# Moving one group's preparation earlier in a hand-ordered DeltaNet and maxout FFN kernel

## Chip, cores and metric

The kernel runs on one core of one Trainium2 chip. The metric is the time of one execution on the device, in microseconds (us). Three runs of the kernel before gave 530.14, 530.81 and 528.37 us; the median is 530.14.

## What is computed

The first part is a delta-rule attention: for each of 4 batches and 8 heads, a 48x48 state is read and updated over 768 time steps. Its output, reshaped to 3072 rows of 384, goes through a feed-forward block with three input matrices, the maximum of the three products, and an output matrix.

```
k_n = k / (norm(k) + 1e-06)
for t in range(S):
    y[:, :, t] = einsum('bhd,bhde->bhe', q[:, :, t], state)
    v_old = einsum('bhde,bhd->bhe', state, kt)
    state = state + bt * einsum('bhd,bhe->bhde', kt, vt - v_old)
x = y.transpose(0, 2, 1, 3).reshape(B * S, H * D)
h = maximum(maximum(x @ w1, x @ w2), x @ w3)
out = h @ w_out
```

The inputs q, k, v and beta are float32; the FFN weights arrive as 64-bit floats and are converted on the chip.

## The kernel before

**Tiling.** Time is cut into 12 chunks of 64 steps. Two chunks make a group (`m`, 0 to 5), and a group gives one FFN tile of 512 tokens. A chunk has two units (`n`, 0 to 23), one for each half of the batches. The diff works on group 2 (units 8 to 11, "the third group"), while group 1 (chunks 2 and 3, units 4 to 7) passes through its recurrence and the FFN runs on group 0.

**What a group needs.**

- `turn(n)` (L345): TensorE transposes k and q of a unit into PSUM (`p_t`), ScalarE copies them to a `kqt` tile (6 buffers). In the tables it is `t`; for a unit of group 1 the q half alone is `T`, and `queries` adds a `load_q(n + 3)` on SyncE (SP) behind it.
- `gram(n)` (L427): TensorE forms K K^T and K Q^T (`p_g`). VectorE masks the q part into `pt` (L422), then ScalarE copies the k part to `at` (L455), and `at` is written to DRAM as `at_d` by four DMAs (L468). For units 10 and 11 these are on POOL's queue, otherwise on SP's. It is `g` in the tables; the q part alone of units 4 to 7 is `P`. `pt`, `at` and the FFN's `h` tiles share 17 "square" buffers.
- `blocks(m)` (L510): one DMA on SP reads `at_d` back as `x_bl`, rearranged into 32x32 blocks, one for each partition.
- `solve(m)` (L521): a generator. Its first step takes the norms from the diagonal of `x_bl` (the root on ScalarE, L261; then VectorE, L262 to L266 and L281; L539 to L541), puts a scaled diagonal in place (POOL, L542) and scales `x_bl` (VectorE, L551). Then come 31 steps of forward substitution, each with one product (L565) and one difference (L569) on VectorE; then the result is written to DRAM as `y_d` (L591, SP) and read back as `ut` in two halves (L600). For group 1, `x_bl` and `y_bl` lie in the not yet used tile `wo_sb`, so the profile calls them that.
- The joins of a chunk: `turn_t1` (`d`, VectorE L632 and L634), `join_z` (`z`, TensorE p_z L709, ScalarE copies L712 and L714) and `join_u` (`j`, TensorE p_j L723, ScalarE L683).
- The recurrence: `old_k` (`k`), `old_q` (`q`), `new` (`u`, p_u L768), `step` (`s`), `to_y` (`y`), `to_x` (`x`).

**The FFN as clock.** `ffn(0)` is a generator of 31 pieces. Pieces 0 to 17 handle 256 tokens, pieces 18 to 26 handle 512: six matmuls each (p_h, L926), into one of two PSUM buffers, which are freed by a ScalarE copy (L934, every third piece) or a VectorE maximum (L940). Pieces 27 to 30 are the output products (p_o, L958). After each piece, the main loop (L1140 to L1178) issues what is listed for its number: weight fetches, `FIRST` (L1096), `EARLY_LINKS` (L1089), one weight conversion (`conv`: three ScalarE instructions L238 to L240, one on VectorE L250, one addition on POOL L254), some substitution steps, and loads. From group 1 on, other tables do the same.

**What sets the order.** The schedule is written by hand (`manual_schedule`, L96): each engine's instructions stand in its queue in the order of the program. Waits between engines are put in by the framework. So the place of a call in the loop fixes what it stands behind on each of the engines and DMA queues it uses. Within one piece the order is: fetches, the opening of `solve(2)`, `FIRST`, `EARLY_LINKS`, the conversion, further substitution steps, the loads, and `blocks(2)`.

Of the kernel before, what the change touches and what calls it, by code (L numbers as in the profile page):

```python
# [23 lines left out]
def kernel(  # L24
# [31 lines left out]
    nc = tc.nc  # L56
# [49 lines left out]
    both_queues = (nc.sync, nc.scalar)  # L106
    one_queue = (nc.sync, nc.sync)

    def rows(bb):
        return slice(C * bb, C * (bb + 1))  # L110
# [6 lines left out]
    def load(src, dst, n, queues):  # L117
        c, g = divmod(n, 2)
        for bb in range(2):
            queues[bb].dma_start(  # L120
                out=dst[rows(bb ^ g), :, 0:D],
                in_=src[2 * bb + g, :, c * C : (c + 1) * C, :].rearrange(
                    "h p d -> p h d"
                ),
            )
# [7 lines left out]
    def load_q(n, queues=one_queue):  # L133
        load(q, qpad[n % NQ], n, queues)

    def load_v(c, queue=nc.sync):
        vts[c] = work.tile([128, 2, H, D], FP32, name="v_t", bufs=3)
        for bb in range(2):
            queue.dma_start(  # L139
                out=vts[c][rows(bb)].rearrange("p g h d -> p (g h) d"),  # L140
                in_=v[2 * bb : 2 * bb + 2, :, c * C : (c + 1) * C, :].rearrange(
                    "b h p d -> p (b h) d"
                ),
            )
# [43 lines left out]
    t1 = [const.tile([128, 2, H, BL], FP32, name=f"t1{i}") for i in range(NU)]  # L188
# [286 lines left out]
    def in_rows(t):  # L475
        return t.rearrange("p s r -> p (s r)")[:, 0 : BL * BL].rearrange(
            "p (j i) -> p j i", i=BL
        )


    def in_wo(i):
        n = BL * BL + BL
        return wo_sb.rearrange("p t d -> p (t d)")[:, n * i : n * (i + 1)].rearrange(
            "p (s r) -> p s r", s=2
        )
# [35 lines left out]
    def solve(m):  # L521


        x = in_rows(xs[m])
        if m == 1:
            y_bl = in_wo(1)
        else:
            y_bl = work.tile([128, 2, HB * BL + HB], FP32, name="y_bl", bufs=1)
            if m > 2:
                zero = kpad[0][:, 0:1, D : D + 1]  # L530
                nc.scalar.copy(y_bl, zero.to_broadcast(y_bl.shape))
            else:
                nc.gpsimd.memset(y_bl, 0.0)
        y = in_rows(y_bl)
        bl = small("bl", BL)
        norm(bl, diagonal(x), small("root_bl", BL), small("nt_bl", BL))
        if m:
            norms_of(m, bl)
        nc.vector.reciprocal(bl, bl)  # L539
        nc.vector.tensor_tensor(out=bl, in0=bl, in1=bl, op=ALU.mult)  # L540
        nc.vector.tensor_tensor(out=bl, in0=bl, in1=beta_bl[:, m] if m else beta_0, op=ALU.mult)  # L541
        (nc.scalar.copy if m > 2 else nc.gpsimd.tensor_copy)(diagonal(y), bl)  # L542
        if m < FINE:
            size, xv, yv = HB, in_blocks(xs[m]), in_blocks(y_bl)
            xb = xv[:, :, :, 0:HB]
            by = bl.rearrange("p (s i) -> p s i", i=HB)[:, :, None, :]
            by = by.to_broadcast([128, 2, HB, HB])
        else:
            size, xv, yv = BL, x[:, None], y[:, None]
            xb, by = x, bl[:, None, :].to_broadcast([128, BL, BL])  # L550
        nc.vector.tensor_tensor(out=xb, in0=xb, in1=by, op=ALU.mult)  # L551
        yield
        for j in range(size - 1):
            a, b = j + 1, size - 1 - j
            n = BL // size
            tmp = work.tile([128, 256], FP32, name="tmp")
            t_v = tmp[:, 0 : n * a * b].rearrange("p (s c i) -> p s c i", s=n, i=b)
            row, column, rest = (
                xv[:, :, j, None, j + 1 : size],
                yv[:, :, 0:a, j, None],  # L560
                yv[:, :, 0:a, j + 1 : size],
            )
            if n == 1:
                row, column, rest, t_v = (t[:, 0] for t in (row, column, rest, t_v))
            nc.vector.tensor_tensor(  # L565
                out=t_v, in0=row.to_broadcast(t_v.shape),
                in1=column.to_broadcast(t_v.shape), op=ALU.mult,
            )
            nc.vector.tensor_tensor(out=rest, in0=rest, in1=t_v, op=ALU.subtract)  # L569
            yield  # L570
        if m == 0:
            back = in_rows(xs[0])
            nc.vector.transpose(out=back, in_=y.rearrange("p c i -> p i c"))
            yield
            for cc in range(2):
                for i in range(4):
                    bb, half = divmod(i, 2)
                    r = block(bb, half)
                    to = ut[cc][r, :, :, BL * half : BL * (half + 1)].rearrange(
                        "p g h i -> p (g h) i"  # L580
                    )
                    of = back[r, :, 16 * cc : 16 * (cc + 1)].rearrange("p i x -> p x i")
                    if half:
                        nc.scalar.copy(to, of)
                    else:
                        (nc.gpsimd if cc else nc.vector).tensor_copy(to, of)
                yield
            return
        y_d = dram.tile([2, 2, B, H, BL, BL], FP32, name="y_d")
        for cc in range(2):  # L590
            nc.sync.dma_start(  # L591
                out=y_d[cc].rearrange("f b h i j -> (f b h) i j"),
                in_=y[64 * cc : 64 * (cc + 1)],
            )
        yield
        for cc in range(2):
            for half in range(2):
                for bb in range(2):
                    r0 = C * bb + BL * half
                    (one_queue if m or cc else both_queues)[bb].dma_start(  # L600
                        out=ut[cc][
                            r0 : r0 + BL, :, :, BL * half : BL * (half + 1)
                        ].rearrange("p g h i -> p (g h) i"),
                        in_=y_d[cc, half, 2 * bb : 2 * bb + 2].rearrange(
                            "b h c i -> c (b h) i"
                        ),
                    )
            yield
# [363 lines left out]
    def some(gen, n):  # L972
        for _ in range(n):
            if next(gen, gen) is gen:
                break

    conv = weights()
    solving = solve(0)
# [96 lines left out]
    for n in (2, 3):  # L1075
        masked(pts[n], by_par(pts[n]))
    load_q(4)
    solving = solve(1)
# [8 lines left out]
        11: "u1 w0", 13: "y1 x1 s1", 14: "X0 w1", 16: "P0", 17: "X1 K0 K1 K2 K3",  # L1087
    }
    EARLY_LINKS = {  # L1089
        9: "k0 q0", 10: "t0", 11: "t1", 12: "g0", 13: "t2", 14: "g1", 15: "t3",  # L1090
        16: "g2", 17: "g3", 19: "d0 d1 z0 z1", 20: "j0", 21: "j1 u0", 22: "s0",
        24: "k1 y0 q1", 25: "u1 x0", 26: "s1", 27: "y1", 29: "x1",
    }


    FIRST = {  # L1096
        0: "f1 s0 S1 S1", 1: "z1 d1 S1 k1 S1 S1", 2: "j1 S1 S1 S1",
        3: "S1 q1 S1 S1", 4: "u1 T4", 5: "y1", 6: "s1 T5", 7: "x1 T6",
        8: "T7", 14: "P4", 15: "P5", 22: "P6", 23: "P7",
    }  # L1100


# [37 lines left out]
    for i, _ in enumerate(ffn(0)):  # L1140
        if 0 < i < 7:
            fetch(nc.sync)
        for _ in range(FETCHED.get(i, 0)):
            fetch(nc.gpsimd if i < 18 else nc.sync)
        if i == 25:
            some(conv, 1)
        if i == 20:
            solving = solve(2)
            some(solving, 1)
        if i == 21:  # L1150
            some(solving, 3)
        queries(FIRST.get(i, ""))
        links(1, EARLY_LINKS.get(i, ""))
        if i in CONVERTED:
            some(conv, 1)
        if 3 < i < 15:
            some(solving, (1, 1, 1, 1, 2, 3, 3, 3, 3, 3, 2)[i - 4])
        if i in (8, 12):
            prep_values(i // 4)
        if i in (1, 7):  # L1160
            for n in range(2):
                load_k(8 + 2 * (i > 1) + n, (nc.gpsimd, nc.gpsimd))
        if i in (1, 3):
            load_q(5 + i // 2)
        if i == 11:
            load_q(11, (nc.gpsimd, nc.gpsimd))
        if i in (3, 8, 10, 22):
            load_v((3, 8, 10, 22).index(i) + 2)
        if i == 18:
            blocks(2)  # L1170
        if i == 23:
            prep_values(4)
        if i > 21:
            some(solving, (3, 2, 3, 2, 2, 5, 5, 5, 4)[i - 22])
        if i in (27, 28, 29):
            load_blocks(i - 15, nc.sync)
        if i > 28:
            less_first(i - 29)  # L1178
# [5 lines left out]
    for m in range(1, GROUPS):  # L1184
        for i, _ in enumerate(ffn(m)):
# [8 lines left out]
            if m + 2 < GROUPS:  # L1194
                if i == 6:
                    blocks(m + 2)
                if i == 8:
                    solving = solve(m + 2)
# [32 lines left out]
```

## Time and profile before

| | |
|---|---|
| median of three runs | 530.14 us |
| the profiled execution | 529.45 us |
| its span in the profile | 527.7 us |
| mean granted TensorE clock | 0.966 |
| TensorE, VectorE, ScalarE, POOL busy | 94%, 59%, 31%, 35% of the span |
| pieces 0 to 17 of `ffn(0)` | 51.3 to 108.4 us |
| pieces 18 to 26 | 109.6 to 149.0 us |
| the output products of group 0 | 150.0 to 167.8 us |

The profile is one execution. Its times count from the span's start. A line of a timeline gives the start, the duration, the engine, the line of code, the instruction with its output and inputs, and how many were merged; what stands in brackets is the idle time of the engine before it and what is taken to have ended it. The chain of waits gives start, duration and instruction, followed back from the last. SPq is the queue of SyncE, which only issues DMAs here.

### The profile page before, as it was taken

How to read it: one execution, taken by the hardware profiler on the slowest of the kernel's cores; microseconds unless marked ns; L12 is line 12 of the kernel's file. 1: busy time of each engine (PE TensorE's matmuls, PEld its weight loads, DVE VectorE, ACT ScalarE, POOL GpSimd, SP SyncE). 2: the span in 40 equal slices, each digit the busy share in tenths (PEclk: the TensorE clock that was granted, in tenths of full speed). 3: DMA queues.
4: the chain of work that ended last, by engine and by line, in shares of the span. 5: the costliest groups of instructions: out<-in, count | busy, mean ns of one | idle time of the engine just before them, and what ended most of it. 6: DMA issues, size and time to landing. Idle time of an engine off the chain costs nothing.

```text
span 527.7 us, 18038 instructions
## 1 busy us (share of the span) xinstructions
PE 495.3 (94%) x7840; PEld 305.5 (58%) x7840; DVE 309.3 (59%) x695; ACT 164.5 (31%) x302; POOL 187.0 (35%) x308
## 2 busy tenths in 40 slices
PE   6666999798999999999999999999999999999996
PEld 6556678654565655556555665555565555654453
DVE  5877999946978664449662888654887231111100
ACT  5557576477311253110142201242201411011000
POOL 6515263653373668812195880501230000000000
PEclk9856899998999999999999999999999999999999
DMA  8974499466036865514594554833334202220011
GB/s 108 200 164 106 101 206 162 128 160 192 2 77 150 168 108 139 129 31 99 112 169 90 141 124 109 163 55 89 88 92 101 43 2 62 53 67 0 0 30 32
DMA packets 109055, 53.47 MB, mean 101 GB/s; under 512 B 91760, under 2 KB 102928, under 8 KB 108976
## 3 DMA queue, kind: packets, MB, share of 16 engines
q1 hardware_dynamic: 98704, 36.79, 33.6%
q0 software_dynamic: 8160, 15.13, 12.9%
q8 instruction: 62, 1.02, 0.8%
q10 hardware_dynamic: 2112, 0.39, 0.5%
q14 instruction: 17, 0.14, 0.1%
HBM read 39.17 MB, written 13.11 MB: 99 GB/s over the span
## 4 chain that ended last, share of the span: by engine, by line
PE 76%; DVE 13%; DMA 4%; ACT 3%; issue 2%; POOL 1%; SPq 0%; ACTq 0%; DVEq 0%
PE p_h L926 33%; PE p_o L958 25%; PE p_g L438 3%; DVE wo_sb L569 2%; PE p_u L768 2%; PE p_k L740 2%; DVE tmp L565 2%; PE p_q L740 2%; PE p_y L810 2%; PE p_s L791 1%; PE p_m L906 1%; DMA qall<-in_q_dram 1%; PE p_j L723 1%; DMA kpad<-in_k_dram 1%; PE p_z L709 1%
## 5 line engine op out<-in xcount | busy, mean ns | idle before, releaser
L926 PE MATMUL p_h<-xt,w_sb 128*128 128x512 f32 (+1 forms) x522 | 220.1, 566 | 9.0 <-DVE h L940 3.8
L926 PEld LDWEIGHTS p_h<-xt,w_sb 128*128 128x128 f32 x522 | 96.4, 194 | 95.7 <-issue 81.1
L958 PE MATMUL p_o<-wo_sb,h 128*128 128x384 f32 x288 | 97.7, 490 | 0.0
L940 DVE TENSOR_TENSOR h<-h,p_h 128x512 f32<-128x512 f32 (+1 forms) x48 | 29.7, 618 | 96.8 <-PE p_h L926 88.3
L958 PEld LDWEIGHTS p_o<-wo_sb,h 128*128 128x128 f32 x288 | 53.8, 190 | 36.0 <-issue 0.5
L964 ACT COPY o_sb<-p_o 128x384 f32<-128x384 f32 x24 | 11.5, 479 | 133.9 <-PE p_o L958 133.9
L565 DVE TENSOR_TENSOR tmp<-x_bl,y_bl 128x31 f32<-128x31 f32 (+20 forms) x139 | 50.3, 362 | 4.1
L569 DVE TENSOR_TENSOR y_bl<-y_bl,tmp 128x31 f32<-128x31 f32 (+20 forms) x139 | 49.2, 354 | 4.8
L936 ACT ACTIVATE h<-p_h 128x512 f32<-128x512 f32 x30 | 17.9, 597 | 91.3 <-PE p_h L926 83.9
L958 PE MATMUL p_o<-w_sb,xt 128*128 128x384 f32 x120 | 42.0, 486 | 0.0
L396 POOL DMA_DIRECT2D turned<-in_q_dram x72 | 39.1, 551 | 4.7 <-POOL turned L391 2.6
L438 PE MATMUL p_g<-kqt 48*64 48x64 f32 (+1 forms) x1216 | 27.3, 237 | 6.5 <-DVE nt_bl L263 3.8
L438 PEld LDWEIGHTS p_g<-kqt 48*64 48x64 f32 x1216 | 24.2, 137 | 13.9 <-ACT kqt L367 7.9
L958 PEld LDWEIGHTS p_o<-w_sb,xt 128*128 128x128 f32 x120 | 22.8, 190 | 15.9
L120 POOL DMA_DIRECT2D kpad<-in_k_dram x32 | 21.8, 689 | 24.9 <-PE p_s L791 23.9
L254 POOL TENSOR_TENSOR w_sb<-mant,up 128x384 int32<-128x384 int32 x18 | 18.2, 1009 | 30.2 <-DVE mant L250 17.1
L287 POOL TENSOR_TENSOR v_t<-v_t,nrm 128x768 f32<-128x768 f32 x12 | 17.9, 1495 | 25.8 <-DVE nrm L266 12.4
L798 DVE TENSOR_TENSOR st<-st,p_s 48x768 f32<-48x768 f32 (+1 forms) x18 | 17.1, 949 | 11.1 <-PE p_s L791 10.9
L812 DVE TENSOR_TENSOR y<-qs,p_y 128x768 f32<-128x768 f32 x11 | 10.5, 953 | 20.2 <-PE p_y L810 20.1
L391 POOL MEMSET turned<- 128x96 f32 x18 | 3.3, 191 | 47.2 <-DVE kqt L412 47.2
L139 POOL DMA_DIRECT2D v_t<-in_v_dram x12 | 9.9, 827 | 28.2 <-PE p_u L768 28.2
L752 DVE TENSOR_TENSOR v_t<-v_t,p_k 128x768 f32<-128x768 f32 x11 | 10.5, 951 | 15.9 <-PE p_k L740 15.9
(152 smaller groups left out, 624.3 us busy)
## 6 DMA issues: line engine op xcount, KB each, us to landing
w_bits<-in_moe_w_dram SPq DMA_DIRECT2D x14, 384.0 KB, 5.2
out_dram<-o_sb SPq DMA_DIRECT2D x48, 96.0 KB, 2.2
turned<-in_q_dram POOLq DMA_DIRECT2D x72, 48.0 KB, 2.8
kpad<-in_k_dram POOLq DMA_DIRECT2D x32, 96.0 KB, 5.3
y_x<-y SPq DMA_DIRECT2D x16, 192.0 KB
qall<-y_x SPq DMA_DIRECT2D x32, 96.0 KB, 2.7
ut<-y_d SPq DMA_DIRECT2D x40, 64.0 KB, 3.4
v_t<-in_v_dram SPq DMA_DIRECT2D x12, 192.0 KB, 6.1
```

The costliest lines, as they stand in the source:

```text
L120: queues[bb].dma_start(out=dst[rows(bb ^ g), :, 0:D], in_=src[2 * bb + g, :, c * C : (c + 1) * C, :].rearrange("h p d -> p h d"),)
L254: nc.gpsimd.tensor_tensor(out=dst.bitcast(I32), in0=mant_v.bitcast(I32), in1=up_v, op=ALU.add)
L287: nc.gpsimd.tensor_tensor(out=vts[c], in0=vts[c], in1=nrm[:, :, :, None].to_broadcast([128, 2, H, D]), op=ALU.mult,)
L396: (queue, nc.gpsimd)[i].dma_start(out=t[p0 : p0 + 32, bb, at : at + NP * 2 * D].rearrange("p (j x) -> p j x", j=NP), in_=(k, q)[i][2 * bb ...
L438: nc.tensor.matmul(p_g[rows(bb ^ (g * i)), par, c0 : c0 + C * (1 + whole)], kq[:, 0], kq if whole else kq[:, i],)
L565: nc.vector.tensor_tensor(out=t_v, in0=row.to_broadcast(t_v.shape), in1=column.to_broadcast(t_v.shape), op=ALU.mult,)
L569: nc.vector.tensor_tensor(out=rest, in0=rest, in1=t_v, op=ALU.subtract)
L740: nc.tensor.matmul(p_b[rows(bb), par, c0 : c0 + D], kqt[g][dims(par), j, bb ^ g, i], st[dims(par), bb ^ g, g, j],)
L926: nc.tensor.matmul(p_h, w_sb[i][:, t, f * 128 : (f + 1) * 128], xt[:, t, lo : lo + w], start=(t == 0), stop=(t == KT - 1),)
L936: nc.scalar.activation(out=h, in_=p_h, func=mybir.ActivationFunctionType.Relu)
L940: nc.vector.tensor_tensor(out=h, in0=h, in1=p_h, op=ALU.max)
L958: nc.tensor.matmul(p_o, stays, moves, start=(n == 0), stop=(n == len(terms) - 1))
```

## The change

Nothing is added to or taken from the computation: the same instructions are issued in another order, and one set of DMAs uses another queue.

- Group 1's `T` (transposes of q) and the loads of q move up: q5 and q6 to pieces 0 and 1, T4 to T7 from pieces 4, 6, 7, 8 to 2, 4, 5, 6, q11 from piece 11 to 8.
- Group 2's transposes move from pieces 10, 11, 13, 15 to 8, 10, 11, 13; its Gram products from 12, 14, 16, 17 to 10, 12, 14, 15; its block read from 18 to 16.
- Group 1's q products P4 to P7 move from pieces 14, 15, 22, 23 to 11, 19, 21, 22.
- `solve(2)` opens at piece 18 and not 20. Its steps: from three right after piece 21 and (3 2 3 2 2 5 5 5 4) from piece 22, to (2 2 2 2 3 3 3 3 5 5 4 1) from piece 19.
- The joins of group 1 and what follows them in the table move up by one piece, to 18 and on; `load_v(5)` from 22 to 21.
- Half of the reads of `ut` for group 1 go to POOL's queue; before, all eight are on SP's.

```diff
-                    (one_queue if m or cc else both_queues)[bb].dma_start(
+                    ((nc.sync, nc.gpsimd) if m == 1 else one_queue)[bb].dma_start(
...
     EARLY_LINKS = {
-        9: "k0 q0", 10: "t0", 11: "t1", 12: "g0", 13: "t2", 14: "g1", 15: "t3",
-        16: "g2", 17: "g3", 19: "d0 d1 z0 z1", 20: "j0", 21: "j1 u0", 22: "s0",
-        24: "k1 y0 q1", 25: "u1 x0", 26: "s1", 27: "y1", 29: "x1",
+        8: "t0", 9: "k0 q0", 10: "t1 g0", 11: "t2", 12: "g1", 13: "t3", 14: "g2",
+        15: "g3", 18: "d0 d1 z0 z1", 19: "j0", 20: "j1 u0", 21: "s0",
+        23: "k1 y0 q1", 24: "u1 x0", 25: "s1", 26: "y1", 28: "x1",
     }
...
     FIRST = {
-        0: "f1 s0 S1 S1", 1: "z1 d1 S1 k1 S1 S1", 2: "j1 S1 S1 S1",
-        3: "S1 q1 S1 S1", 4: "u1 T4", 5: "y1", 6: "s1 T5", 7: "x1 T6",
-        8: "T7", 14: "P4", 15: "P5", 22: "P6", 23: "P7",
+        0: "f1 s0 S1 S1", 1: "z1 d1 S1 k1 S1 S1", 2: "T4 j1 S1 S1 S1",
+        3: "S1 q1 S1 S1", 4: "T5 u1", 5: "T6 y1", 6: "s1 T7", 7: "x1",
+        11: "P4", 19: "P5", 21: "P6", 22: "P7",
     }
...
-        if i == 20:
+        if i == 18:
             solving = solve(2)
             some(solving, 1)
-        if i == 21:
-            some(solving, 3)
         queries(FIRST.get(i, ""))
         links(1, EARLY_LINKS.get(i, ""))
...
-        if i in (1, 3):
-            load_q(5 + i // 2)
-        if i == 11:
+        if i in (0, 1):
+            load_q(5 + i)
+        if i == 8:
             load_q(11, (nc.gpsimd, nc.gpsimd))
-        if i in (3, 8, 10, 22):
-            load_v((3, 8, 10, 22).index(i) + 2)
-        if i == 18:
+        if i in (3, 8, 10, 21):
+            load_v((3, 8, 10, 21).index(i) + 2)
+        if i == 16:
             blocks(2)
...
-        if i > 21:
-            some(solving, (3, 2, 3, 2, 2, 5, 5, 5, 4)[i - 22])
+        if i > 18:
+            some(solving, (2, 2, 2, 2, 3, 3, 3, 3, 5, 5, 4, 1)[i - 19])
```

## The prediction

> **What bounds the kernel now.** I read the page first, then TensorE's order of time with its idle spells, then VectorE, SyncE and the chain of waits around them. "Piece i" is the i-th step of the generator `ffn(0)`.
>
> ```profile
> PE 495.3 (94%) x7840; PEld 305.5 (58%) x7840; DVE 309.3 (59%) x695; ACT 164.5 (31%) x302; POOL 187.0 (35%) x308
> ```
>
> TensorE is busy 94% of 527.7 us. Of its idle time, only that between 58 and 127 us lies where the change works; from 131 us to the end it hardly stops (0.70, 0.34 and 0.37 us in all). So a delay of TensorE at 131 us is a delay of the end.
>
> ```profile
> 92.74 1.56 PE L926 MATMUL p_h<-xt,w_sb 128*128 128x256 f32 x6 [1.01 <-DVE h L940]
> ...
> 100.68 1.56 PE L926 MATMUL p_h<-xt,w_sb 128*128 128x256 f32 x6 [2.42 <-DVE h L940]
> ...
> 109.58 5.42 PE L926 MATMUL p_h<-xt,w_sb 128*128 128x512 f32 x12
> 114.93 1.37 PE L709 MATMUL p_z<-ut,at 32*32 32x32 f32 x128
> 116.44 2.81 PE L926 MATMUL p_h<-xt,w_sb 128*128 128x512 f32 x6
> 119.19 0.75 PE L723 MATMUL p_j<-z,t 32*32 32x32 f32 x64
> ...
> 126.81 3.35 PE L926 MATMUL p_h<-xt,w_sb 128*128 128x512 f32 x4 [2.29 <-DVE tmp L565]
> ```
>
> Counting the groups of six, 92.74 is piece 13, 100.68 piece 15, 109.58 pieces 18 and 19, 126.81 piece 22. Up to 103 us VectorE is behind: it shows no idle spell from 57 to 105 us, and the maxima that free PSUM stand in its queue behind the substitution of group 1. From 109.58 TensorE leads until the unexplained hole before piece 22.
>
> ```profile
> 107.01 4.88 SPq L600 DMA_DIRECT2D ut<-y_d  x8
> 111.94 0.96 SPq L215 DMA_DIRECT2D w_bits<-in_moe_w_out_dram  x2
> 117.96 0.33 SPq L515 DMA_DIRECT2D x_bl<-at_d  x1
> ```
> ```profile
> 112.97 1.65 POOL at_d L468 x3
> 114.63 3.27 DMA at_d<-at
> 117.90 0.02 SPq L515
> 117.96 3.84 DMA x_bl<-at_d
> 121.80 0.02 issue
> 121.83 0.27 ACT root_bl L261
> ```
>
> This is the chain that decides: the last Gram block of group 2 is copied by ScalarE at 110.56 (its row), written out by POOL, lands at 117.90, is read back, lands at 121.80; 11.2 us in all. Only then do `solve(2)`'s root and norms run.
>
> ```profile
> 116.33 0.69 DVE L940 TENSOR_TENSOR h<-h,p_h 128x512 f32<-128x512 f32 x1 [5.66 <-ACT h L934]
> 116.93 0.44 DVE L632 STREAM_TRANSPOSE t<-ut 128x256 f32<-128x256 f32 x1
> ...
> 122.12 0.18 DVE L262 TENSOR_SCALAR nt_bl<-root_bl 128x32 f32<-128x32 f32 x1 [1.42 <-ACT root_bl L261]
> ...
> 125.16 1.22 DVE L551 TENSOR_TENSOR x_bl<-x_bl,bl 128x1024 f32<-128x1024 f32 x1
> ```
>
> VectorE runs d0, d1 and the maxima of pieces 19 and 20 (to 120.7) before these norms. The wait for x_bl has little behind it.
>
> [...] TensorE reads `ut` at 114.93, so it had landed, yet its transpose on VectorE starts at 116.93, behind the maximum that waited 5.66 us. [...] after the 2.29 us hole the granted clock is 0.54 over 126 to 129 us; after the 2.42 us one at 100.68 it stayed 1.00. [...] Here 3.27 us for the last block's write, and SP stood until it landed. [...]
>
> **The change, part by part.**
>
> Front moves. T4 to T7, t0 and q5 to q11 go up one to three pieces. TensorE does the same work (0.44 us per 4 transposes). SP still interleaves these loads with weight fetches that wait for conversions; q4 and q5 were issued at 50.41 and 52.71, ten microseconds ahead of the new T4, so its data is there. POOL's q11 load (1.42 us) moves from 94.03 into POOL's idle 6.46 us before 89.35. I cost these at 0: VectorE's full queue to 103 us hides them. Without that cover the late q's would cost one load, 3 us.
>
> Gram work. Before, one masked pass (g0) stands in VectorE's queue ahead of the last step of `solve(1)`; after, three (g0, P4, g1). Two passes at 0.59 us from start to start: +1.18. The last step ends at 102.62 + 1.18 = 103.8, piece 15 starts near 101.8, y_d is issued 103.9. Behind it stand two passes instead of four: g2 at 104.0, g3 at 104.9. ScalarE copies g2's block near 104.7, then three conversions and h (1.9 us), then g3's near 107.1, against 108.67 and 110.56. P5 goes to piece 19; it was the one square buffer too many, so h of piece 18 no longer waits for the join (115.71). Pieces 16 to 18 (1.4, 1.4, 2.77 us, g3's 1.1 beside) end near 111.2 instead of 112.3: 1.1 us gained here.
>
> Queues. y_d lands 4.3 us after issue as before (102.68 to 107.01): 108.2. Half the `ut` reads now sit on POOL, between g2's and g3's writes. POOL: g2's four writes 105.2 to 107.7 (2.44), a conversion 1.0 to 108.7, four ut reads at about 0.6, no row for this pair, bounds 0.58 (L468) and 0.69 (q and k loads), I take 0.65: to 111.3; g3's writes 2.35 to 113.6. Landing: 2.0 to 2.7 us after the last issue's end (before 2.7, with two weight loads beside it): 116.1 taken at 2.5. x_bl: 3.0 to 3.84 us (4096-byte rows, alone then as now): near 119.6, bounds 118.5 to 122. So the read-back comes 2.2 us sooner, not two to four pieces. The ut reads land near 113 to 114, 1 us sooner than 114.9, but they are wanted at 111.2: p_z waits some 2 us, which lies inside the next wait and adds nothing.
>
> The added wait. `solve(2)` opens at piece 18, ahead of d0 d1 z0 z1 in the program. Its root therefore stands on ScalarE ahead of the z copies, its norms on VectorE ahead of d0 and d1, and ahead of the maxima of pieces 19 and 20. Behind the root: z copies (p_j waits for them), conversions, h of piece 21. Ahead of the root stand the conversions of pieces 16 and 17, which wait for POOL's add behind g3's writes (114.6), and h of piece 18: to about 118, hidden by x_bl. Behind the norms: d0 (p_j waits), d1, then the PSUM of piece 19. Root at 119.6, norms from root to the end of L551 126.38 - 121.83 = 4.5 us: 124.1; d0 (0.44 + 0.90) 1.4 us: p_j at 125.5. TensorE has only p_z, piece 19 and P5 for that time, done near 118: idle 7 us.
>
> Sum. I count to the end of piece 22's matmuls, before at 131.03. After: p_j 125.5, then j0 0.68, piece 20 2.77, j1 0.68, u0 1.08, pieces 21 and 22 5.54: 136.25. That is +5.2. The old 2.29 us hole and its half-clock piece (4.21 instead of 2.77) are in 131.03 and so given back already. [...] I take +1.7. P6, P7, s0, k1 and so on are the same work in another order: 0; VectorE has 12 steps instead of 9 in pieces 23 to 26 (0.85 us each), against a TensorE that is late, bound 0 to +2, taken 0. `load_v(5)`, one piece sooner on SP behind the fetches, 0 (needed a group later). At the end: the steps finish a piece sooner, so `less_first` runs in time for group 1's first matmul, which idled 0.70 at 168.44: -0.7. Total +6.2: 529.45 (the profiled execution, span 527.7) + 6.2 = 535.7. The median of the three runs is 530.14, 0.7 above that execution; I keep the smaller base.
>
> **Rivals.** (B) Milder: POOL keeps pace and loads land at their quickest, x_bl near 116.5. p_j at 122.4, +2.1, half clock +0.3 on average, -0.7: 531.2. For: ScalarE's copy is 3.5 us sooner. Against: POOL's ut reads stand in between. (C) Faster: x_bl is there by the end of piece 18, as the change means. Then the hole (2.29), its half clock (1.44) and the 0.70 go: 529.45 - 4.4 = 525.0. For: those waits exist. Against: the chain of 11.2 us would have to start near 100 us, and VectorE can't reach g3's mask before 104.9. (D) Worse than forecast: [...] x_bl at 122 (+2.4), VectorE's denser steps (+1): 541. C is the other side's: it decides from an x_bl landing before about 113 us; from 115 on the wait eats it.
>
> **Chances.** 0.5% of 530.14 is 2.65 us, about what a measurement of this kernel can tell from no change. Forecast 0.60 (533 to 539), B 0.15, C 0.10, D 0.15. Faster 0.10 (C), same 0.15 (B), slower 0.75. Leaving out C and the upper half of D, the range is 529.5 to 541.5.
>
> **What would show it.** Right: ScalarE's root waits for x_bl for some 2 us or more (from h of piece 18) with the z copies right behind it; VectorE idle until about 120, then norms, then L632; p_j about 125; TensorE idle 5 us or more after P5, then clock 0.5; POOL's four ut reads between the two groups of L468. Wrong: x_bl lands before 115; or p_z, p_j and piece 20 follow without a gap; or the time moves for something outside 85 to 175 us.

## The result

The kernel after takes 543.13 us (median of four runs, 541.52 to 543.98); the kernel before, with one more run beside it, 530.19 (528.37 to 530.81). The ratio is 1.0246, with a 95% interval of 1.0208 to 1.0284: the change makes the kernel 12.9 us slower. The prediction was 535.7 us with a range of 529.5 to 541.5, so the sign is right, but 543.13 lies outside the range, and less than half of the loss was foreseen.

The page of the kernel after, its first line of engines:

```profile
PE 502.4 (93%) x7840; PEld 309.9 (57%) x7840; DVE 309.5 (57%) x695; ACT 164.6 (30%) x302; POOL 189.9 (35%) x312
```

TensorE has the same 7840 matmuls and is busy 502.4 us instead of 495.3: so seven microseconds of the loss are the same work taking TensorE longer, at a mean granted clock of 0.952 instead of 0.966. Only POOL has more instructions, the four `ut` reads. The profiled execution took 543.98 us, its span is 542.3.

| in the profile, us | before | after | difference | predicted difference |
|---|---|---|---|---|
| first matmul of `ffn(0)` | 51.29 | 52.43 | +1.14 | 0 |
| VectorE's maximum of piece 10 | 88.58 | 89.74 | +1.16 | 0 |
| `y_d` issued | 102.68 | 108.05 | +5.37 | +1.2 |
| `x_bl` issued | 117.96 | 119.57 | +1.61 | -1.9 |
| `x_bl` landed (start + duration of the read) | 121.80 | 124.38 | +2.58 | -2.2 |
| first p_j of chunk 2 | 119.19 | 129.45 | +10.26 | +6.3 |
| end of piece 22 | 131.03 | 143.2 | +12.2 | +6.9 |
| group 1's first FFN matmul | 168.44 | 179.63 | +11.2 | +6.2 |
| group 2's first FFN matmul | 255.94 | 270.12 | +14.2 | +6.2 |
| profiled execution | 529.45 | 543.98 | +14.5 | +6.2 |

The end of piece 22 after is its end in the trace, 144.76, less 1.55 for P6 and s0, which now stand ahead of it. In the last prediction column 6.9 is 5.2 + 1.7, and 6.2 takes off the gap of 0.70. After group 2's first matmul nothing more is lost but 0.3 us.

The first row does not belong to the change. It stands ahead of every instruction that the change moves:

```profile
51.29 2.90 PE L926 MATMUL p_h<-xt,w_sb 128*128 128x256 f32 x6 [1.94 <-DVE xt L877]
```
```profile
52.43 1.53 PE L926 MATMUL p_h<-xt,w_sb 128*128 128x256 f32 x6 [1.26 <-DVE xt L877]
```

The upper line is before, the lower after. In the nine kernels below that keep the same start, this matmul stands between 51.04 and 52.84 us. So profiled executions differ by up to 1.8 us at this place already, and the 1.16 us of the second row are this same difference, carried along by VectorE's full queue.

TensorE of the kernel after in order of time, around the change (start, duration, instruction; idle time before it in brackets):

```profile
88.27 1.08 PE L438 MATMUL p_g<-kqt 48*64 48x128 f32 x27
92.59 0.44 PE L438 MATMUL p_g<-kqt 48*64 48x128 f32 x5 [3.23 <-issue]
...
118.77 1.06 PE L709 MATMUL p_z<-ut,at 32*32 32x32 f32 x60 [1.66 <-DMA ut<-y_d]
119.77 5.19 PE L926 MATMUL p_h<-xt,w_sb 128*128 128x512 f32 x6
...
129.45 1.90 PE L723 MATMUL p_j<-z,t 32*32 32x32 f32 x64 [3.87 <-DVE t L632]
131.27 4.56 PE L926 MATMUL p_h<-xt,w_sb 128*128 128x512 f32 x6
```

Three things are to be seen. In the middle of one Gram product, 27 matmuls done and 5 to go, TensorE stands 3.23 us, and the profile names no instruction that it waits for. Behind P5, ahead of the first p_j, it stands 3.87 us for VectorE's transposes. And pieces 19 and 20 take 5.19 and 4.56 us where a piece at full clock took 2.84 before. Piece 19 and P5 end near 125.6, though, and p_j has to wait for VectorE until 129.45 anyway, so the slow piece 19 only made that wait shorter and cost nothing by itself.

ScalarE, then VectorE of the kernel after, from the landing of `x_bl`:

```profile
124.40 0.26 ACT L261 ACTIVATE root_bl<-x_bl 128x32 f32<-128x32 f32 x1 [1.91 <-DMA x_bl<-at_d]
124.57 0.56 ACT L712 COPY z<-p_z 32x512 f32<-32x512 f32 x1
```
```profile
124.69 0.18 DVE L262 TENSOR_SCALAR nt_bl<-root_bl 128x32 f32<-128x32 f32 x1 [4.42 <-ACT root_bl L261]
...
128.86 0.44 DVE L632 STREAM_TRANSPOSE t<-ut 128x256 f32<-128x256 f32 x1
```

This is the predicted queue order, line for line: the root ahead of the z copies, the norms ahead of L632, and everything behind the landing of `x_bl`. Before, L632 stood at 116.93 and did not wait for it.

SyncE, then POOL of the kernel after:

```profile
108.05 1.15 SPq L591 DMA_DIRECT2D y_d<-wo_sb  x2
112.01 1.91 SPq L600 DMA_DIRECT2D ut<-y_d  x4
119.57 0.34 SPq L515 DMA_DIRECT2D x_bl<-at_d  x1
```
```profile
109.83 2.42 POOL L468 DMA_DIRECT2D at_d<-at  x4 [1.72 <-ACT at L455]
...
113.20 2.58 POOL L600 DMA_DIRECT2D ut<-y_d  x4
115.77 2.31 POOL L468 DMA_DIRECT2D at_d<-at  x4
```

POOL's order is also as forecast, with 0.645 us (2.58 by 4) for one `ut` read where 0.65 was taken; but its first line starts at 109.83 and not at 105.2. All these lines are of one execution: run 7 below has the same program up to its output pieces, and there the root starts at 123.12 and the first p_j at 128.17, 1.3 us sooner.

### The profile page after: what moved, and what is told of

It is laid out like the page before. It is cut to its first block, busy times and chain, and to the rows that moved or that the text cites. A ratio compares the mean times of both kernels' runs of the same rounds, so it can differ in the third digit from the quotient of the medians.

```text
span 542.3 us, 18031 instructions
## 1 busy us (share of the span) xinstructions
PE 502.4 (93%) x7840; PEld 309.9 (57%) x7840; DVE 309.5 (57%) x695; ACT 164.6 (30%) x302; POOL 189.9 (35%) x312
## 3 DMA queue, kind: packets, MB, share of 16 engines
q8 instruction: 62, 1.02, 0.8%
## 4 chain that ended last, share of the span: by engine, by line
PE 72%; DVE 10%; issue 5%; DMA 4%; ACT 4%; POOL 3%; SPq 2%; DVEq 0%; POOLq 0%; ACTq 0%
PE p_h L926 31%; PE p_o L958 22%; PE p_g L438 4%; PE p_u L768 3%; PE p_y L810 2%; PE p_s L791 2%; PE p_k L740 2%; PE p_m L906 1%; PE p_j L723 1%; PE p_q L740 1%; DVE wo_sb L569 1%; PE p_t L361 1%; DVE tmp L565 1%; DMA kpad<-in_k_dram 1%; DMA x_bl<-at_d 1%
## 5 line engine op out<-in xcount | busy, mean ns | idle before, releaser
L926 PE MATMUL p_h<-xt,w_sb 128*128 128x512 f32 (+1 forms) x522 | 222.7, 572 | 4.4 <-DVE h L940 1.5
L565 DVE TENSOR_TENSOR tmp<-x_bl,y_bl 128x31 f32<-128x31 f32 (+20 forms) x139 | 51.7, 372 | 4.1
L936 ACT ACTIVATE h<-p_h 128x512 f32<-128x512 f32 x30 | 17.9, 597 | 90.2 <-PE p_h L926 82.8
L438 PE MATMUL p_g<-kqt 48*64 48x64 f32 (+1 forms) x1216 | 29.8, 249 | 9.9 <-DVE nt_bl L263 3.8
L438 PEld LDWEIGHTS p_g<-kqt 48*64 48x64 f32 x1216 | 26.2, 148 | 18.9 <-issue 8.4
L422 DVE TENSOR_TENSOR pt<-p_g,mask 128x512 f32<-128x512 f32 x20 | 13.8, 688 | 12.1 <-PE p_g L438 12.1
## 6 DMA issues: line engine op xcount, KB each, us to landing
v_t<-in_v_dram SPq DMA_DIRECT2D x12, 192.0 KB, 12.6
```

The lines of the kernel that those rows point to most:

```text
L438: nc.tensor.matmul(p_g[rows(bb ^ (g * i)), par, c0 : c0 + C * (1 + whole)], kq[:, 0], kq if whole else kq[:, i],)
L565: nc.vector.tensor_tensor(out=t_v, in0=row.to_broadcast(t_v.shape), in1=column.to_broadcast(t_v.shape), op=ALU.mult,)
L926: nc.tensor.matmul(p_h, w_sb[i][:, t, f * 128 : (f + 1) * 128], xt[:, t, lo : lo + w], start=(t == 0), stop=(t == KT - 1),)
L936: nc.scalar.activation(out=h, in_=p_h, func=mybir.ActivationFunctionType.Relu)
```

## The experiments

**Theories.** Q: the loss is made by queue order; the norms of `solve(2)`, opened at piece 18, hold the joins until `x_bl` lands. F: it is made by the front; TensorE's spells marked "issue" and the later substitution delay `x_bl`. T: it is made behind 145 us, where the new list of steps puts DMAs of `solve(2)` on SyncE ahead of the next loads (the expectation of run 7 calls it the second part of Q). I, beside F: such a spell belongs to the place of an instruction in TensorE's stream, not to what it computes. Ratios are against the kernel before on the same chip; the runs were spread over several chips, so medians of different kernels are compared only roughly.

**1. The opening back at piece 20**, with before's list of steps.

```diff
-        if i == 18:
+        if i == 20:
...
+        if i == 21:
+            some(solving, 3)
...
-        if i > 18:
-            some(solving, (2, 2, 2, 2, 3, 3, 3, 3, 5, 5, 4, 1)[i - 19])
+        if i > 21:
+            some(solving, (3, 2, 3, 2, 2, 5, 5, 5, 4)[i - 22])
```

> The changed kernel, with only the opening of solve(2) and its steps put back to where they were before (opened at piece 20). Theory Q (the root and norms of solve(2) stand in ScalarE's and VectorE's queues ahead of the joins, so the joins wait for x_bl): p_j comes within 2 us of p_z and piece 19, near 124 instead of 129.45, no half-clock stretch after it, and y_d is again written behind the block loads; 533 to 535 us. Theory F (the loss comes from the front, where TensorE and VectorE are 5 us late by 108 us, and from the ut reads): 539 to 543 us.

Measured: 535.64 us, 1.0112 [1.0054, 1.0170], a little above what Q expected; 7.5 of the 12.9 us come back. The first p_j is at 124.15, group 1's FFN at 171.36. Of what remains, TensorE's waits for `ut` in p_z are a visible part (0.77 and 1.41 us before 117 us, and this one):

```profile
189.40 0.88 PE L709 MATMUL p_z<-ut,at 32*32 32x32 f32 x64 [1.81 <-DMA ut<-y_d]
```

**2. The opening at 18, but behind the joins of that piece.** The same instructions as after; the block that opens `solve(2)` stands two lines lower.

```diff
+        queries(FIRST.get(i, ""))
+        links(1, EARLY_LINKS.get(i, ""))
         if i == 18:
             solving = solve(2)
             some(solving, 1)
-        queries(FIRST.get(i, ""))
-        links(1, EARLY_LINKS.get(i, ""))
```

> The changed kernel, solve(2) still opened at piece 18, but behind d0 d1 z0 z1 of the same piece instead of ahead of them; its steps unchanged. Theory Q: z copies and d0 no longer wait for x_bl, p_j near 124; only the maximum of piece 19 still stands behind the norms (to 129), which costs about 1 us; the late end of group 1's loads stays: 535 to 538 us. Theory F: no change, 542 to 544 us.

Measured: 537.15 us, 1.0131 [1.0075, 1.0187], 6 us better than after. VectorE of this kernel:

```profile
120.61 0.43 DVE L632 STREAM_TRANSPOSE t<-ut 128x256 f32<-128x256 f32 x1
...
125.52 0.18 DVE L262 TENSOR_SCALAR nt_bl<-root_bl 128x32 f32<-128x32 f32 x1 [2.14 <-ACT root_bl L261]
```

Nothing but an order differs, L632 comes 8.2 us sooner (128.86 to 120.61), and group 1's FFN starts at 172.97 instead of 179.63. This is the cleanest proof of Q, and it also says that Q is not all: 4.5 us of delay are left at group 1's FFN (168.44 before), and some 3 us more are lost behind that point (below, 7).

**3. All `ut` reads on SyncE**, the rest as after.

```diff
-                    ((nc.sync, nc.gpsimd) if m == 1 else one_queue)[bb].dma_start(
+                    (one_queue if m or cc else both_queues)[bb].dma_start(
```

> The changed kernel with all eight reads of ut back on SP's queue. Theory Q with POOL's queue as its longest link: POOL writes the last Gram block some 2.5 us sooner, x_bl lands near 122 instead of 124.4, p_j near 127; ut lands 2 us later without cost: 540 to 541.5 us. If the reads on POOL don't matter: 543 us; if the later ut decides: 544 us or more.

Measured: 538.79 us, 1.0162 [1.0110, 1.0215], better than expected; the interval still touches that of the kernel after. POOL's second group of writes goes out at 112.88 instead of 115.77, `x_bl` is issued at 117.38 instead of 119.57, the root follows at 121.02 instead of 124.40, the first p_j at 126.50. So with the norms ahead of the joins, what delays `x_bl` delays the joins. Of the 3.4 us at the root, 2.2 come from the issue of the read; the other 1.2 come from a shorter read (3.64 us from issue to root, where after has 4.83), which this edit doesn't explain.

**4. The other way round: only the `ut` reads split, in the kernel before.** It is the diff of 3 reversed.

> The kernel before with only the ut reads split over SP and POOL. Theory Q: ut lands about 1.5 us sooner, where nobody waits for it, and POOL has its conversions and Gram writes 0 to 2 us later: 529.5 to 532 us, no difference that can be measured. If the split itself were a loss: 533 us or more.

Measured: 530.36 us, 1.0013 [0.9993, 1.0034]: no change. In its profile `x_bl` is issued at 120.44 instead of 117.96, and the time is the same: POOL's four reads cost nothing while nothing that waits for `x_bl` stands ahead of the joins.

**5 and 6. TensorE's stream shifted.** At the start, behind the warming matmuls, 32 small matmuls are added, whose product is used nowhere; once in the kernel before, once in after.

```diff
+    p_w = ps_ffn([128, TOK], "p_w")[0:32, 0:32]
+    for _ in range(32):
+        nc.tensor.matmul(p_w, ident[0:32, 0:32], ident[0:32, 0:32])
```

> The kernel before with 32 small extra matmuls into a scratch PSUM tile behind the warm-up matmuls, about 128 TensorE instructions, 0.5 to 1 us of work while TensorE waits for the first loads. It tests what ended TensorE's idle spell of 2.29 us ahead of piece 22. Theory I (TensorE ran out of instructions there, and the 16 KB fetches on the instruction queue fall at fixed places in its stream): the spell moves or shrinks with the places of the fetches, and the time changes by 1 to 4 us either way. Theory W (a wait on VectorE): the spell stays where it is, and the time is 530 to 531 us.

> The changed kernel with the same 32 small extra matmuls at the start. Theory I: the 3.23 us spell in the middle of unit 8's Gram products (27 of 32 matmuls done) goes from there, VectorE gets its mask at 89.7 instead of 93.1 and y_d is written about 3 us sooner; x_bl and p_j come up to 3 us sooner: 540 us, between 538 and 543 by where the next fetch falls. Theory W: the spell stays, 543 to 544 us.

Measured: 538.0 us (1.0124 [1.0082, 1.0166]) and 555.32 us (1.0458 [1.0424, 1.0492]). Both times missed what was expected. TensorE of the shifted kernel before:

```profile
42.72 1.49 PE L691 MATMUL p_f<-z,t 64*64 64x32 f32 x42 [3.70 <-issue]
```

The added matmuls alone took 3.62 us (at 4.86) where half a microsecond to one was expected, and the first matmul of `ffn(0)` stands at 58.05 instead of 51.29, or 56.91 instead of 52.43. In the kernel before this start is nearly all of the loss, so its time says nothing about the spells. The shifted kernel after lost 12 us by the medians (the profile is of the fastest execution, 549.88); beyond the 4.5 us at the start this stayed unexplained.

For theory I the places count. In before the large spells stood at 44.01 (0.97) and 58.95 (0.41); shifted, one of 3.70 us stands at 42.72. In after, shifted, the spell in unit 8's Gram product is gone; one of 1.15 us stands at 92.54 in p_q, and others of 0.83 and 1.59 us at 202 to 208 us. The count itself can be read from the traces. The spell of after comes behind 3,475 of TensorE's records (matmuls and weight loads), and so it does in all eight kernels here that have after's front, with 2.24 to 3.39 us. In both shifted kernels a spell (0.96 and 1.15 us) comes behind 3,477 records, though by the added matmuls other instructions stand there. So the place follows the count of TensorE's instructions, not the product that is computed. The size can't be told from this.

The hole of 2.29 us ahead of piece 22, which the first of these runs was to test, is not in the shifted kernel (0.91 and 0.29 us in its place). It is not in run 4 either, whose TensorE stream is that of before (0.32, 0.29 and 0.27 us), so it can't be laid to the shift; the forecast had counted this hole of one execution as given back.

**7. The last two numbers of the list of steps exchanged**, so that the write of `y_d` and the reads of `ut` come a piece later.

```diff
-            some(solving, (2, 2, 2, 2, 3, 3, 3, 3, 5, 5, 4, 1)[i - 19])
+            some(solving, (2, 2, 2, 2, 3, 3, 3, 3, 5, 5, 1, 4)[i - 19])
```

> The changed kernel with the last four yields of solve(2) (last step, y_d written, ut read in two halves) in piece 30 instead of 29, so behind the loads of unit 14's blocks on SP's queue, as before. Theory Q's second part (those loads now stand behind the y_d write and the ut reads on SP; VectorE waits 3.1 us for them in group 1's FFN and its join transposes come late): the idle spells of 1.04 us at 199.8 and the half-clock stretch behind them go: 540 to 541 us. If that order doesn't matter: 543 us.

Measured: 541.82 us, 1.0210 [1.0184, 1.0236], 1.3 us better than after by the medians, but the two intervals overlap. SyncE of the kernel before, then SyncE of the kernel after and what follows on its VectorE and on its TensorE:

```profile
166.38 3.86 SPq L396 DMA_DIRECT2D kmore<-in_k_dram  x8
...
171.54 2.42 SPq L591 DMA_DIRECT2D y_d<-y_bl  x2
175.33 4.88 SPq L600 DMA_DIRECT2D ut<-y_d  x8
```

```profile
182.95 6.64 SPq L600 DMA_DIRECT2D ut<-y_d  x8
189.69 3.77 SPq L396 DMA_DIRECT2D kmore<-in_k_dram  x8
```
```profile
194.92 0.45 DVE L412 STREAM_TRANSPOSE kqt<-kmore 128x256 f32<-128x256 f32 x1 [1.77 <-DMA kmore<-in_k_dram]
```
```profile
199.77 0.21 PE L723 MATMUL p_j<-z,t 32*32 32x32 f32 x2 [0.54 <-DVE t L632]
...
202.65 4.54 PE L926 MATMUL p_h<-xt,w_sb 128*128 128x512 f32 x6
```

The reads of k, 23 us later than before where group 1's FFN is 11 us later, hold VectorE 1.77 us here and 1.30 us at 196.67; behind them stand the join transposes; TensorE idles 1.04 us in three bits (0.54, 0.25, 0.25), and the piece behind these runs at a mean granted clock of 0.61 (4.54 us instead of 2.84). With the two numbers exchanged, `kmore` is issued at 178.57 and these lines are gone, but `ut` is read later and p_z waits 1.57 us for it at 196.34. From group 1's first FFN matmul to group 2's it takes 87.50 us before, 90.49 after, 88.69 here: 1.8 of T's 3.0 us. The same stretch is 90.2 to 90.5 us in kernels 2, 3 and 8, which keep after's list of steps, and 87.2 in 9 and 10, which keep before's list and before's joins.

The list of steps alone does not make the tail, though. Kernels 1 and 11 have before's list, but the joins a piece sooner, and take 88.8 and 91.4 us; there p_z waits for `ut` as in this run. In these three kernels `y_d` is issued 5.8 us behind group 1's first FFN matmul, in before, 9 and 10 only 3.1 us. So the moved joins have a part in the tail, and no run has them without the rest.

**8. Unit 8's Gram product ahead of unit 9's transposes.**

```diff
-        8: "t0", 9: "k0 q0", 10: "t1 g0", 11: "t2", 12: "g1", 13: "t3", 14: "g2",
+        8: "t0", 9: "k0 q0", 10: "g0 t1", 11: "t2", 12: "g1", 13: "t3", 14: "g2",
```

> The changed kernel with the two calls of piece 10 swapped (unit 8's Gram products ahead of unit 9's transposes; no instruction more or less). If TensorE's 3.23 us spell is a missing block of instructions at a fixed place of its stream, it now falls 70 instructions behind piece 10 as before, which is inside the transposes, and VectorE has its mask before it: y_d near 105 instead of 108, x_bl near 121.5, p_j near 126.5: 539.5 to 541.5 us. If the spell comes from the Gram products themselves: 543 us.

Measured: 541.79 us, 1.0209 [1.0176, 1.0242]. The spell did not go with g0; it now stands in the transposes:

```profile
92.12 0.37 PE L361 MATMUL p_t<-ident,kpad 128*128 128x128 f32 x1 [2.36 <-issue]
```

`y_d` is issued at 107.10 instead of 108.05; 105 was expected. A second finding for I: other instructions in the same place of the stream (behind the same 3,475 records), a spell again.

**9. The front of the change alone.** Kernel after with the parts of 1 and 3 undone, the joins, P6, P7 and `load_v(5)` at before's pieces, and P5 at 20.

```diff
-        15: "g3", 18: "d0 d1 z0 z1", 19: "j0", 20: "j1 u0", 21: "s0",
-        23: "k1 y0 q1", 24: "u1 x0", 25: "s1", 26: "y1", 28: "x1",
+        15: "g3", 19: "d0 d1 z0 z1", 20: "j0", 21: "j1 u0", 22: "s0",
+        24: "k1 y0 q1", 25: "u1 x0", 26: "s1", 27: "y1", 29: "x1",
...
-        11: "P4", 19: "P5", 21: "P6", 22: "P7",
+        11: "P4", 20: "P5", 22: "P6", 23: "P7",
```

> The changed kernel's early part alone (T4 to T7, q loads, group 2's transposes, Gram products and block read, P4 and P5), with joins, solve(2), its steps, P6, P7, load_v(5) and the ut reads at the places of before (P5 in piece 20). Theory Q: no root and no norm stands ahead of a join, so what remains is VectorE's late y_d (5 us): p_z waits 2 to 3 us for ut: 531 to 533.5 us. Theory F (the early part is where the loss comes from): 538 us or more.

Measured: 532.08 us, 1.0044 [1.0019, 1.0069]: slower by 2.2 us. TensorE of this kernel:

```profile
91.67 0.44 PE L438 MATMUL p_g<-kqt 48*64 48x128 f32 x5 [2.79 <-issue]
...
105.15 2.93 PE L926 MATMUL p_h<-xt,w_sb 128*128 128x256 f32 x6 [2.75 <-DVE h L940]
...
124.74 0.75 PE L723 MATMUL p_j<-z,t 32*32 32x32 f32 x64
```

The spell is there, and a wait of 2.75 us for VectorE's late maximum follows, behind which the piece takes 2.93 us where 1.56 was taken at 97.63, and the 64 Gram matmuls behind it 2.05 us (1.22 at 96.48). The wait of p_z for `ut` that was expected did not come. The first p_j does not wait for the norms (no bracket).

**10. The opening alone.** Kernel before with only `solve(2)`'s first step at piece 18 and `blocks(2)` at 17.

```diff
-        if i == 20:
+        if i == 18:
             solving = solve(2)
...
-        if i == 18:
+        if i == 17:
             blocks(2)
```

> The kernel before with only the opening of solve(2), its first step, moved from piece 20 to piece 18, and the block read from piece 18 to 17 so that it is issued ahead of it; steps from piece 21 on as before, joins at piece 19 as before. Theory Q: the joins' copies and transposes stand behind root and norms, p_j near 127.5 instead of 119.2, TensorE idle 7 us before it and at half clock after: 534 to 537 us. Theory F: 530 us.

Measured: 538.98 us, 1.0146 [1.0110, 1.0183], 9.1 us above before by the medians and 2 us more than Q expected. ScalarE, VectorE, TensorE of this kernel:

```profile
122.52 0.26 ACT L261 ACTIVATE root_bl<-x_bl 128x32 f32<-128x32 f32 x1 [4.63 <-DMA x_bl<-at_d]
```
```profile
122.81 0.18 DVE L262 TENSOR_SCALAR nt_bl<-root_bl 128x32 f32<-128x32 f32 x1 [10.55 <-ACT root_bl L261]
...
127.58 0.44 DVE L632 STREAM_TRANSPOSE t<-ut 128x256 f32<-128x256 f32 x1
```
```profile
128.17 0.28 PE L723 MATMUL p_j<-z,t 32*32 32x32 f32 x2 [7.32 <-DVE t L632]
```

The whole chain of the prediction in its pure form: ScalarE waits for the DMA, VectorE for ScalarE, TensorE for VectorE, 7.32 us in one hole, and then a granted clock of 0.50 (125 to 135 us).

**11. Three parts undone together** (1, 3 and 8), the joins still one piece sooner than before.

> The changed kernel with three things at once: solve(2) and its steps at the places of before, all ut reads on SP, and Gram products ahead of the transposes in piece 10; joins one piece sooner as in the change. Theory Q: what is left is the wait of p_z for ut (y_d 2 to 3 us late, the join a piece early), some 3 us: 531 to 534 us. If the three parts don't add up: 535 us or more.

Measured: 536.73 us, 1.0119 [1.0070, 1.0168], no better than 1 alone, and not the 531 to 534 that Q expected. Its TensorE waits 2.41 us for `ut` at 189.93, and the piece behind that wait takes 4.35 us instead of 2.84 (at 191.13); its spell in p_t is 3.24 us. So the parts don't add up, and why was not settled.

## Why the prediction was wrong in size

The forecast for the profiled execution was +6.2 us, and +14.5 came. Of the missing 8.3 us, 4.0 are there at the first p_j of chunk 2 (129.45 instead of 125.5), 1.3 more at the end of piece 22, and 3.0 come between the first FFN matmuls of groups 1 and 2. The mechanism that the forecast put first, the joins behind the norms, was right; the steps below had the wrong size or were not counted.

The parts were also measured by themselves: +9.1 for the opening (run 10), +2.2 for the front (run 9), and 1.3 that run 7 gave back. Their sum, 12.6, is near the 12.9 of the medians, but that doesn't prove that the parts add. Run 1 undoes the opening and the list of steps and should then stand 2.2 us above before; it stands 6.2 above (535.64 to 529.45), and run 11 is no better. What both keep and run 9 does not are the joins, P5 to P7 and `load_v(5)` one piece sooner; what these cost was not measured by itself.

**What held.** That the place of the opening is the largest part, and how: root ahead of the z copies, norms ahead of d0, d1 (runs 2 and 10). The two masks at +1.18. POOL's order, and 0.65 us for a `ut` read. p_z's wait for `ut`: some 2 us were forecast, 0.73 + 1.66 came. That the wait of p_z lies inside the next one and adds nothing: piece 19 and P5, behind it, end near 125.6, and p_j stands until 129.45. Rival C, the faster one, was tied to `x_bl` landing before about 113 us; it landed at 124.4.

**Right by luck, or not at all.** The gap of 0.70 us at group 1's first matmul went, but not for the reason given (that the steps finish sooner). In before that matmul waits for ScalarE's copy of an output:

```profile
168.44 2.81 PE L926 MATMUL p_h<-xt,w_sb 128*128 128x512 f32 x6 [0.70 <-ACT o_sb L964]
```

The gap is gone in runs 1 and 11 too, whose steps are those of before, and stays 0.70 in runs 9 and 10, whose joins are those of before. So, as far as these runs show, it goes with the moved joins. And `h` of piece 18, which was to come by 118, comes at 121.92, behind conversions that wait for POOL (before, 115.71); the landing of `x_bl` hides it, as the forecast said.

**First failed step: "near 119.6, bounds 118.5 to 122" for the landing of x_bl.** It is 124.4, beyond the upper bound. 3.5 us of the 4.8 are there when the read is issued (119.57, where the forecast's 2.5 us of landing gave 116.1), and they begin with the last substitution step: `y_d` is issued at 108.05, not at 103.9. Of these 4.15 us, 1.16 are the later start of this execution, which the change didn't make. Some 3 are the spell in unit 8's Gram product, which VectorE's mask has to wait for:

```profile
93.08 0.69 DVE L422 TENSOR_TENSOR pt<-p_g,mask 128x512 f32<-128x512 f32 x1 [2.92 <-PE p_g L438]
```

The forecast said of the front moves "I cost these at 0: VectorE's full queue to 103 us hides them", and counted the two masks at +1.18 with no wait. The cover was real for all that TensorE does late, except for g0: VectorE's queue has the mask of g0 right behind the maximum of piece 10, and so VectorE itself waits for TensorE. The rest, 1.3 us, is the read: 4.81 us where some 3.5 was taken. "Alone then as now" was wrong for both kernels; SyncE issues weight fetches right behind it, four before (3.84 us) and five after while the read is under way. Their number doesn't decide: in runs 3 and 7, with five as well, it is 3.6 and 3.7 us from issue to root. So this 1.3 us is spread of one execution as far as the runs show; without it, as in run 7, the landing of about 123.1 is still beyond the bound by 1.1 us, 0.9 of which are the later start of that execution.

**Second: half clock, counted at +1.7.** The 1.7 was the author's estimate. Stretches of the kernel after (us from : to, length, busy of TensorE, its loads, VectorE, ScalarE, POOL, granted clock, DMA share, GB/s), and the same of before:

```profile
118.00:124.80 6.80, 6.03 (x66) 2.78 (x66) 0.67 (x2) 3.77 (x9) 3.95 (x5) 0.52 0.65 214
128.00:135.00 7.00, 5.31 (x69) 2.98 (x70) 6.46 (x14) 2.73 (x5) 2.09 (x2) 0.52 0.06 21
202.70:207.10 4.40, 4.40 (x9) 1.81 (x8) 0.72 (x3) 1.18 (x2) 0.61 (x2) 0.61 0.48 84
```
```profile
126.50:130.00 3.50, 3.19 (x4) 1.44 (x5) 2.37 (x8) 2.43 (x5) 1.84 (x2) 0.55 0.60 107
```

There are two long stretches at a clock of 0.52, not one, and a third at 203 us in the tail. Only what stands on the critical path counts. The first stretch slows piece 19 (5.19 us), but p_j waits for the norms anyway, so it costs nothing. The second, behind the wait for the norms, is the term that was forecast: from p_j to the end of piece 22 it is 13.75 us, where 10.75 was the work, so 3.0 us and not 1.7; nearly all of it is in p_j (1.90 us where it took 0.75 before) and in piece 20. The third makes the piece at 202.65 take 4.54 us, 1.7 above 2.84; before, the piece at 126.81 lost 1.4.

The first stretch begins inside p_z's wait for `ut`. In runs 1, 3 and 11 the piece behind p_z's waits is slow too (5.49, 5.49 and 4.51 us instead of 2.84); in 2, 7 and 8, with single waits of up to 0.9, 1.2 and 1.3 us there, it takes 2.84, and in run 9, where TensorE doesn't wait there, the granted clock is 1.00 from 115 to 135 us. So the wait can bring the stretch and need not. In the profiles of before and after the granted clock changes only at multiples of 3.41 us from its first change. And the same hole of 2.42 us ahead of piece 15 was followed by a piece of 1.56 us in before and by one of 2.93 in run 4. The hole of 3.87 us went with 6.8 us at half clock (after), that of 7.32 with 10.2 (run 10: a mean of 0.98 over 120 to 125 us, then 0.50 to 135); and that of 2.75 in run 9 was followed by at least 7.3 us at about half speed (2.93, 2.05 and 2.50 us for six, 64 and five matmuls, to 112.5). The shortest stretches at half clock around here, 126.22 to 129.64 in before and 203.03 to 206.44 in after, are 3.41 us long, and half of that is 1.7. So the 1.7 stood for the shortest stretch and not for the middle.

**Third: the sum ended at -0.7 for the tail.** I did not follow the moved steps' DMAs past SyncE's queue in the output pieces: the last yields of `solve(2)` carry two writes and eight reads, and these now stand ahead of the k loads of a later unit. Nor did I follow what the moved joins do there (run 7). That term is +3.0 in the profile, beside the -0.7. Run 7 shows 1.8 of it for the order of these DMAs; for the rest, that it comes with the joins is read from runs 1 and 11 and not shown alone. I had counted `y_d` and `ut` in the middle of the kernel, for group 1, and not at its end, for group 2.

Rival D (541) had another 1.7 us for half clock and `x_bl` at 122; it was the nearest, and both terms were right in kind. It had neither the spells nor the tail.

**The spells.** What the trace shows: the queue marked "instruction" moves 62 packets, 1.02 MB in all, so 16 KB each. The DMA view of the kernel after for 89 to 90 us (packets, MB, share of 16 engines):

```profile
q8 instruction: 1, 0.02, 9.7%
```

One packet of that queue falls into the spell: it starts at 89.69 and takes 1.55 us (9.7% of 16 engines in 1 us). The kernel after has five spells (0.27 to 3.23 us) for its 62 packets, before has three (0.34 to 0.97), and run 5 has one of 3.70 us; so most packets come without one. That TensorE stands for want of what such a packet brings is the author's reading, and no run shows it directly. Two things fit it. The spells keep their place in the count (runs 5, 6, 8), and in all eight of these spells of before and after TensorE goes on 1.2 to 1.7 us after the end of such a packet. For the 3.23 us these are 91.24 and 92.59. Between 84 and 88 us the profile gives the DMA engines a busy share of 1.25; whether that makes the packet late was not shown, for no run took those loads away. That the spell delays `y_d` by some 3 us is read from VectorE's wait of 2.92 us. Runs 6 and 8 bear it out in part: there VectorE waits 1.6 and 1.7 us for TensorE in all, and `y_d` is issued 54.6 and 54.7 us behind the first matmul of `ffn(0)`, where it is 55.6 after and 51.4 before. No run with after's front is without such a wait.

**Open.** The size of a spell beforehand; what the joins one piece sooner cost alone, in the middle and in the tail; why run 11 is no better than run 1; why the shifted kernel after lost 12 us; and how much of run 7's gain (1.3 us by the medians, 1.8 in the stretch) is spread.

## What to carry to other kernels

Before a step is opened sooner, list for every engine what will stand behind its first waiting instruction; if a neighbour on the critical path is among it, put the step behind it in the program, for the order alone was worth 6 us here (run 2). Follow a moved step to its last yield: its DMAs at the end pass other loads on the queue, too, and here that had a part in the 3 us that were lost in group 1's FFN. And price half clock by what stands behind it: of three slow pieces one cost nothing, since the next wait covered it, and the stretch on the critical path cost 3.0 us where 1.7 had been taken. Before a difference of one profile is laid to a change, look whether it is there ahead of the first moved instruction: 1.1 us were, here.

## What the runs showed of the hardware

Thirty-two 32x32 fp32 matmuls in one place of the array, with the same output, took 3.62 us at the kernel's start, 113 ns for each (the profile counts 64, two for each fp32 product). TensorE was slow there in general: the 64 Gram matmuls right behind them took 1.99 us, and 1.18 in the kernel after at 10.01. So this is no price to take elsewhere: the 64 of p_j, 32x32 too, took 0.75 us in before, at a granted clock of 1.00.

TensorE stands for up to 3.70 us with no wait that the profile names, at places that keep to the count of its instructions: behind 3,475 records in eight kernels, and behind 3,477 when matmuls are added thousands of records earlier. In before and after it goes on 1.2 to 1.7 us after a packet on the instruction queue has ended. In the profiles of these two the granted clock changed only at multiples of 3.41 us from its first change. A wait of 1.04 us in three bits, around small products, was followed in after by a piece of 4.54 us at a mean granted clock of 0.61 (202.7 to 207.1), and a single hole of 2.42 us was followed by a piece of 2.93 us in run 4 and of 1.56 in before. A DMA issue of a 64 KB read took 0.51 us on SyncE in run 3 (4.08 for 8), 0.61 in before (4.88 for 8), and 0.65 us on POOL.
